# Row sums moved ahead of the remainder's product with v, and the order and PSUM banks of the score units written out by hand

## The chip, the cores and the metric

The kernel runs on one core of one Trainium2 chip. The metric is the device time of one execution in microseconds (us), the median of three runs. All engines of the core run at once: PE (TensorE, the matrix engine, with its weight loads shown as PEld), DVE (VectorE), ACT (ScalarE), POOL (GpSimd) and SP, which issues DMA transfers.

## The reference

Three stages follow one another; the change touches the first.

```
q_rot, k_rot = rotate(q), rotate(k)              # 4 batches x 8 heads, 576 positions, 64 wide
scores = q_rot @ k_rot^T / 8
attn   = exp(scores - max(scores)) / (sum(exp(scores - max(scores))) + 1e-9)
x      = attn @ v                                # heads side by side: 4 x 576 x 512
x      = moe(x)                                  # x @ w_in, gelu, spatial gate, @ w_out
out    = moe2(x)                                 # gated x @ w_val, @ w_out2
```

## The kernel before

**Attention.** The 32 heads are worked in 16 pairs, `i` = 0 to 15, one after the other. For a pair, PE first forms scores from which only the row maxima are taken, one pair ahead; then it forms the scores again, transposed, with the maximum subtracted inside the product, and ACT takes the exponential of each result straight out of PSUM.

One iteration of the loop in `attention()` has three parts on PE:

1. `phase(i)`: 16 units, in an order given by a string with one letter each. `t` (`st_unit`, lines 654 to 664) is 8 matmuls of pair `i` that make the scores of 128 keys times 288 queries for two heads; ACT's exponential (line 675) empties its bank. `T` (line 670) is the unit of the last 64 keys. `x` and `y` (`s_unit`, line 610) are score products of pair `i+1`, of four matmuls with 256 columns and of two matmuls with 320 columns; DVE's maximum (line 613) empties their bank. `S` (line 620) is the maximum unit of the last 64 queries, emptied by line 622. There are 8 `t`, 1 `T`, 2 `x`, 4 `y`, 1 `S`; the last pair has only the `t` and `T`.
2. `pv_unit` (line 699, eight matmuls in each of four calls): the product of the exponentials with v for the first 512 keys; then `pv_unit` with `(8,)` (line 709): the same for the 64 remaining keys. Both add into one bank, which ACT copies to `xu` (line 713, its copy shows as L263).
3. `sum_unit` (line 733): the row sums of the exponentials, by matmuls with ones, into another bank; ACT reads it into `ss` (line 737). Part of the addition is done ahead by POOL (`ac`, line 260).

**PSUM.** There are four buffers `PS[0]` to `PS[3]`, called banks here (each is in fact two banks wide, one for each head or half). Each unit of a phase takes one of them, and PE may write it only when the engine that empties it is done.

**What sets the order.** All work is put in a list of tasks. Tasks of PE run in exactly the order in which they are added; those of ACT, DVE, POOL and SP are ordered by a planner (class `Plan`) that lists them by modelled costs and due times. In `phase` a small model inside the loop (`free`, `pe`, `ac`, `dv`) chooses the bank for each unit. For the strings that stand there it gives plain rotation: banks 0, 1, 2, 3, 0, 1, ... for the phases 0 to 14 and 0, 1, 2, 0, 1, 2, ... for the last; the product with v is always in bank 3 and the row sums always in bank 2.

At the end of a phase and behind it, `prep_high(i+2)` lets DVE rotate the raw q and k of the pair after next; ACT casts them to `qp`, `qh` and `kh`, and the first `y` of the next phase needs `kh`.

**Behind attention** come the dense products of the two mixers (line 840), which take the time from about 236 us to the end.

Of the kernel before, what the change touches and what calls it, by code (L numbers as in the profile page):

```python
# [21 lines left out]
B, HP, S, DM, HALF = 4, 4, 576, 512, 288  # L22
NPAIR = B * HP
# [139 lines left out]
PASS = 0.132  # L163
MAXIMA = ((0.238, 1.14), (0.146, 0.75))
FP32 = 0.48
PART = 384
MORE = 4


@with_exitstack  # L170
def mixer_kernel(ctx: ExitStack, tc: tile.TileContext, qk, v, vrem, cs, w_in, g_ln, w_sgT, b_sg,
# [25 lines left out]
    PS = [psum.tile([128, 2, 512], F32, name=f"ps{j}") for j in range(4)]  # L197
# [64 lines left out]
    def acopy(out_, in_, n, r, w, after=()):  # L262
        return add("Act", act(n), lambda: nc.scalar.copy(out_(), in_()), r, w, after)  # L263
# [412 lines left out]
    def adds(i):  # L676
        return 4 if FOUR <= i < NPAIR - 1 else 2
# [8 lines left out]
            else:  # L686
                tt("P", lambda: AC[kc], lambda: AC[kc], lambda: E[n], ALU.add, S, [("e", n)], [("ac", kc)])

    def pv_unit(i, us):

        j2 = i % 2
        pv, kp = PS[3], ("ps", 3)
        if us[0] < 8:
            j = UNITS[us[0]][0]

            def mm():
                for h in range(2):
                    for hf in range(2):
                        nc.tensor.matmul(pv[64 * hf:64 * hf + 64, h, 0:HALF], VM[j2][:, j, h], E[EU[i, us[hf]]][:, h],  # L699
                                         start=j == 0, stop=False, skip_group_check=True)  # L700
            add("PE", 2 * FP32 + (0.2 if not j else 0.0), mm, [*[("e", EU[i, u]) for u in us], ("vm", j2)], [kp])
            return
        e = E[EU[i, 8]]

        def mm():
            for hf in range(2):
                for h in range(2):
                    rows = slice(64 * h, 64 * h + 64)
                    nc.tensor.matmul(pv[64 * hf:64 * hf + 64, h, 0:HALF], VR[j2][rows], e[rows, hf], start=False, stop=True,  # L709
                                     skip_group_check=True)  # L710
        add("PE", FP32 + 0.1, mm, [("e", EU[i, 8]), ("vr", j2)], [kp])
        xu = XU[j2]
        acopy(lambda: xu, lambda: pv[:, :, 0:HALF], S, [kp], [("xu", j2)])

        def st(q):
            for hf in range(2):
                q.dma_start(out=xu_d[i // HP][i % HP, :, HALF * hf:HALF * hf + HALF].rearrange("(h d) c -> d h c", h=2),
                            in_=xu[64 * hf:64 * hf + 64])
        dma(290, st, [("xu", j2)], [("xu_d", i)], n=2)

    def sum_unit(i, ps, kps):

        j2 = i % 2
        src = [(ones, ones, [(E[EU[i, u + hf]], h) for h in range(2) for hf in range(2)], ("e", EU[i, u]),
                ("e", EU[i, u + 1])) for u in (4, 6)[adds(i) // 2 - 1:]]
        src.append((ones, ones, [(AC[hf], h) for h in range(2) for hf in range(2)], ("ac", 0), ("ac", 1)))
        e = EU[i, 8]
        src.append((*ones_b, [(E[e], hf) for h in range(2) for hf in range(2)], ("e", e)))

        def mm():  # L730
            for n, x in enumerate(src):
                for t, (a, y) in enumerate(x[2]):
                    nc.tensor.matmul(ps[32 * t:32 * t + 32, 0, 0:HALF], x[t // 2], a[:, y], start=n == 0,  # L733
                                     stop=n == len(src) - 1, skip_group_check=True)
        add("PE", len(src) * FP32 + 0.15, mm, [*[k for x in src for k in x[3:]], ("consts",)], [kps])
        ss, rc = SS[0], RC[j2]
        add("Act", act(HALF), lambda: nc.scalar.activation(ss, ps[:, 0, 0:HALF], AF.Copy, bias=1e-9), [kps], [("ss", 0)])

        def rows(q):
            q.dma_start(out=rc, in_=ss[0:97:32].rearrange("t (p c) -> t p c", c=9))  # L740
        dma(5, rows, [("ss", 0)], [("rc", j2)])
# [22 lines left out]
    def attention():  # L764
        keep_busy(16)
        first_pairs()

        def phase(i, vl):

            order = "ytyttxtttyttyxTS" if i + 1 < NPAIR else "ttttttttT"  # L770
            if not i:
                order = "xtttyttytyttyxTS"
            free = [0.0, 0.0, 0.74 if i else 0.0, 0.0]
            pe, ac, dv = 0.2, 0.0, 0.0
            nt, xs, ys = 0, iter(range(2)), iter(range(2, 6))
            for x, what in enumerate(order):
                ks = range(4) if x < len(order) - 4 else range(3)
                at_once = [k for k in ks if free[k] <= pe]
                k = max(at_once, key=lambda k: free[k]) if at_once else min(ks, key=lambda k: free[k])
                pe = max(pe, free[k])  # L780
                if what in "tT":
                    pe += 4 * PASS if what == "t" else 8 * PASS + 0.24
                    act_at = max(ac, pe + 0.22)
                    ac, free[k] = act_at + 0.55, act_at + 0.75
                    st_unit(i, nt, PS[k], ("ps", k))
                    add_unit(i, nt)
                    nt += 1
                else:
                    pe += 2 * PASS if what == "S" else MAXIMA[what == "y"][0]
                    dve_at = max(dv, pe + 0.29)  # L790
                    dv = dve_at + (0.67 if what == "S" else MAXIMA[what == "y"][1])
                    free[k] = dv + 0.15
                    s_unit(i + 1, {"x": xs, "y": ys, "S": iter((8,))}[what].__next__(), PS[k], ("ps", k))
                if not x:
                    first = [P.last_pe, *vl]
                    if 2 <= i + 1 < NPAIR:
                        prep_low(i + 1, first)
                if x == (12 if i < FOUR else 0):
                    job_s(i, [P.last_pe])
            if i + 1 < NPAIR:  # L800
                s_end(i + 1)

        vl = []
        for i in range(NPAIR):
            if i + 2 < NPAIR:
                prep_load(i + 2)
            if i and i + 1 < NPAIR:
                load_v(i + 1)
            if i:
                job_loads(i)  # L810
            phase(i, vl)
            ep.append(P.last_pe)
            rot = [P.last_pe]
            if 0 < i < FOUR or i == NPAIR - 1:
                sum_end(i - 1, [*rot, *P.writer.get(("mn", (i + 1) % 2, 1), ())] if i + 1 < NPAIR else ())
            if i + 2 < NPAIR:
                rot = prep_high(i + 2, [P.last_pe, *P.writer[("mn", (i + 1) % 2, 1)]])
            vl = job_v(i, [P.last_pe], rot)
            if FOUR <= i < NPAIR - 1:
                sum_end(i - 1, P.writer["kl", (i + 1) % 3])  # L820
            for us in ((0, 2), (1, 3), (4, 5), (6, 7), (8,)):
                pv_unit(i, us)
            sum_unit(i, PS[2], ("ps", 2))
        sum_end(NPAIR - 1)

    def unit(cost, mm, r, new=True):
# [173 lines left out]
    def x2_part(b, dds=range(4)):  # L1000
        j = b % 2
        for dd in dds:
            dc = slice(128 * dd, 128 * dd + 128)
            x2t, kx = ((XS[0], ("xs", 0)), (XS[1], ("xs", 1)), (RB[0], ("rb", 0)), (RB[1], ("rb", 1)),
                       *((y, ("xm", y)) for y in range(MORE)))[nx[0] % (4 + MORE)]
            nx[0] += 1
# [29 lines left out]
    def val_part(b0):  # L1036

        for dd in range(4):
# [5 lines left out]
            def bank(y, z=z):  # L1044
                return PS[z[y // 2]][:, y % 2, 0:PART]

            for ks in ((0, 1), (2,), (3,)):
                def mm(dc=dc, bank=bank, ks=ks):
                    product(3, bank, lambda p, k, y: w2("v", p)[:, k, dc],
                            lambda q, k, y: (T["xh2"], T["xl2"])[q][:, k].rearrange("p a b -> p (a b)")[:, PART * y:PART * y + PART], ks=ks)  # L1050
                add("PE", len(ks) * 9 * 0.1735, mm, [("X2", j, k, m) for j in range(2) for k in ks for m in "hl"]
# [5 lines left out]
            for y in range(2):  # L1057
                n = (2 * PART, PART)[y]

                def part(y=y, n=n, gt=gt):  # L1060
                    return gt()[:, 2 * PART * y:2 * PART * y + n].rearrange("p (a b) -> p a b", b=PART)
                add("DVE", dve(n), lambda y=y, z=z, part=part: nc.vector.tensor_tensor(
                    part(), PS[z[y]][:, 0:2 - y, 0:PART], part(), ALU.mult), [("ps", z[y])], kg[y:])
            for j in range(2):
# [81 lines left out]
    def close_a():  # L1146
# [9 lines left out]
        T["ob"] = [p2.tile([128, 2, 512], F32, name=f"ob{j}") for j in range(2)]  # L1156
        T["xm"] = [p2.tile([128, 4 + S], F32, name=f"xm{j}") for j in range(MORE)]
        for t in T["xm"]:
# [6 lines left out]
        + [("YR", j, k, m) for j in range(B) for k in range(4) for m in "hl"] + [("ob", j) for j in range(2)]  # L1165
        + [("xm", j) for j in range(MORE)])})
    load_g(1)
# [73 lines left out]
```

## Time and profile before

| | us |
|---|---|
| median of 3 runs | 552.12 |
| lowest, highest | 551.88, 552.69 |
| time of the profiled execution | 552.56 |
| its span, first to last instruction | 550.8 |
| PE busy in it | 541.4 (98%) |
| DVE, ACT, POOL busy | 411.7, 278.4, 247.5 |

The span is counted within the profiled execution; the 1.76 us between span and time lie ahead of the first instruction and behind the last. Matmuls are pipelined, and each is shown longer than the distance to the next: a matmul of 288 columns is drawn as 0.29 us and the next pair starts 0.13 us later. PE that waits for a bank can therefore look busy all the while, and the distance from start to start has to be read.

### The profile page before, as it was taken

To read this page: it belongs to the slowest core of one execution; us is meant where nothing else is said; L and a number is where in the kernel's file an instruction comes from. 1 tells how busy PE (TensorE), PEld (TensorE's weight loads), DVE (VectorE), ACT (ScalarE), POOL (GpSimd) and SP (SyncE) were. 2 spreads that over 40 slices of the span, in tenths; PEclk is the share of its full clock that TensorE was granted. 3 is DMA by queue.
4 is the path that set the end of the run, shared out by engine and by line. 5 is a ranking of instruction groups with operands and counts; after the bars stand their busy time and mean duration, and the time that the engine had idled before them with its cause. 6 is when DMAs were issued, how large, how long until landed. Compare 5 with 4: busy or idle time off the path is not lost.

```text
span 550.8 us, 11758 instructions
## 1 busy us (share of the span) xinstructions
PE 541.4 (98%) x4592; PEld 463.3 (84%) x4592; DVE 411.7 (75%) x595; ACT 278.4 (51%) x451; POOL 247.5 (45%) x229
## 2 busy tenths in 40 slices
PE   6999999999999999999999999999999999999996
PEld 5877777777777777679989989989999998899985
DVE  7878888888888888969768556654979997649610
ACT  3567766776666667635526136134157543334221
POOL 5545555555555555456967677554610011222000
PEclk9999999999999999999999999999999999999999
DMA  5565656565666664774484762643264211110022
GB/s 187 141 195 142 184 152 175 160 185 153 188 171 160 168 198 103 214 223 111 131 295 119 231 189 75 196 142 124 104 208 128 73 44 72 44 58 1 0 77 96
DMA packets 58024, 77.39 MB, mean 141 GB/s; under 512 B 29392, under 2 KB 34000, under 8 KB 57968
## 3 DMA queue, kind: packets, MB, share of 16 engines
q1 hardware_dynamic: 57664, 76.37, 46.8%
q8 instruction: 36, 0.59, 0.4%
q10 hardware_dynamic: 304, 0.26, 0.1%
q14 instruction: 20, 0.16, 0.1%
HBM read 55.94 MB, written 18.95 MB: 136 GB/s over the span
## 4 chain that ended last, share of the span: by engine, by line
PE 96%; DVE 2%; DMA 1%; ACT 0%; issue 0%; SPq 0%; ACTq 0%; DVEq 0%
PE ps L840 55%; PE ps L662 12%; PE ps L699 12%; PE ps L733 6%; PE ps L670 4%; PE ps L610 4%; PE ps L709 2%; PE ps L951 2%; DVE raw L259 1%; DVE mx L613 1%; DMA raw<-qk 1%; PE ps L620 1%; DVE mn L622 0%; ACT ob L263 0%; ACT kh L263 0%
## 5 line engine op out<-in xcount | busy, mean ns | idle before, releaser
L613 DVE TENSOR_REDUCE mx<-ps 128x2 f32<-128x640 f32 (+1 forms) x96 | 89.1, 957 | 28.8 <-PE ps L610 21.9
L675 ACT ACTIVATE e<-ps 128x576 f32<-128x576 f32 x144 | 87.0, 652 | 20.3 <-PE ps L670 10.9
L699 PE MATMUL ps<-e,vm 128*64 128x288 f32 x512 | 65.6, 409 | 0.0
L699 PEld LDWEIGHTS ps<-e,vm 128*64 128x64 f32 x512 | 35.3, 137 | 24.7 <-issue 2.6
L260 POOL TENSOR_TENSOR ac<-e,e 128x576 f32<-128x576 f32 x32 | 45.2, 1431 | 9.4 <-ACT e L675 9.4
L840 PE MATMUL ps<-s_h,vn 128*128 128x288 f32 x256 | 46.9, 295 | 0.0
L259 DVE TENSOR_TENSOR raw<-raw,cst 128x1152 f32<-128x1152 f32 (+1 forms) x33 | 42.0, 1272 | 0.5 <-DMA raw<-qk 0.5
L263 ACT CAST qp<-raw 128x512 fp32r<-128x512 f32 x16 | 18.6, 1164 | 45.2 <-DVE raw L259 45.2
L840 PEld LDWEIGHTS ps<-s_h,vn 128*128 128x128 f32 x256 | 38.3, 188 | 0.0
L662 PE MATMUL ps<-qh,kh 64*128 64x288 f32 x256 | 38.3, 295 | 0.0
L662 PE MATMUL ps<-qh,kl 64*128 64x288 f32 x256 | 37.9, 292 | 0.0
L662 PE MATMUL ps<-ql,kh 64*128 64x288 f32 x256 | 37.8, 292 | 0.0
L662 PE MATMUL ps<-mr,one_r 64*128 64x288 f32 x256 | 37.7, 290 | 0.0
L260 POOL TENSOR_TENSOR vs<-vs,u 128x576 f32<-128x576 f32 x16 | 27.0, 1688 | 19.3 <-DVE vs L955 16.8
L610 PE MATMUL ps<-kh,qp 64*128 64x320 f32 (+1 forms) x256 | 32.7, 312 | 2.3 <-ACT kh L263 2.2
L1032 DVE SCALAR_TENSOR_TENSOR gt<-xm,cw,gt 128x576 f32<-128x576 f32 x32 | 28.9, 909 | 1.8 <-ACT gt L1029 1.4
L610 PEld LDWEIGHTS ps<-kh,qp 64*128 64x128 f32 x256 | 21.7, 184 | 10.0 <-ACT kh L263 7.7
L309 DVE TENSOR_SCALAR wt<-wt 128x256 f32<-128x256 f32 (+1 forms) x28 | 16.4, 586 | 16.5 <-ACT wt L319 16.5
L260 POOL TENSOR_TENSOR xl<-xs,xh 128x576 fp32r<-128x576 f32 x2 | 5.3, 2633 | 50.0 <-ACT xh L263 50.0
L840 PE MATMUL ps<-XL,w_h 128*128 128x288 f32 x128 | 27.4, 296 | 0.0
L840 PE MATMUL ps<-XH,w_l 128*128 128x288 f32 x128 | 27.4, 295 | 0.0
L840 PE MATMUL ps<-XH,w_h 128*128 128x288 f32 x128 | 27.4, 295 | 0.0
(181 smaller groups left out, 1493.4 us busy)
## 6 DMA issues: line engine op xcount, KB each, us to landing
raw<-qk SPq DMA_DIRECT2D x31, 576.0 KB
xu_d<-xu SPq DMA_DIRECT2D x32, 144.0 KB
rb<-r_d SPq DMA_DIRECT2D x32, 144.0 KB
xs<-xu_d SPq DMA_DIRECT2D x16, 288.0 KB
x_d<-xs SPq DMA_DIRECT2D x16, 288.0 KB
g_d<-vs SPq DMA_DIRECT2D x16, 288.0 KB
vm<-v SPq DMA_DIRECT2D x16, 256.0 KB
wr<-w_in SPq DMA_DIRECT2D x8, 512.0 KB
```

The lines of the kernel that those rows point to most:

```text
L259: return add("DVE", dve(n), lambda: nc.vector.tensor_tensor(out_(), a(), b(), op), r, w, after, lock=True)
L260: return add("Pool", pool(n), lambda: nc.gpsimd.tensor_tensor(out_(), a(), b(), op), r, w, after, lock=True)
L263: return add("Act", act(n), lambda: nc.scalar.copy(out_(), in_()), r, w, after)
L610: nc.tensor.matmul(ps[:, h, w * y:w * y + w], QP[j2][rows, c], kh[rows, keys], start=True, stop=True)
L613: add("DVE", MAXIMA[n // 2 > 0][1], lambda: nc.vector.tensor_reduce(out=MX[j2][:, n // 2 > 0, :, chunks[0]:chunks[-1] + 1], in_=ps[:, :, 0 ...
L662: nc.tensor.matmul(ps[:, h, 0:HALF], x[rows, keys] if o < 3 else x[rows], y[rows, cols], start=o == 0, stop=o == 3)
L670: nc.tensor.matmul(ps[:, hf, 0:HALF], x, y[:, cols], start=o == 0, stop=o == 3)
L675: add("Act", 0.62, lambda: nc.scalar.activation(E[n], ps[:, :, 0:HALF], AF.Exp), [kps], [("e", n)])
L699: nc.tensor.matmul(pv[64 * hf:64 * hf + 64, h, 0:HALF], VM[j2][:, j, h], E[EU[i, us[hf]]][:, h], start=j == 0, stop=False, skip_group_chec ...
L733: nc.tensor.matmul(ps[32 * t:32 * t + 32, 0, 0:HALF], x[t // 2], a[:, y], start=n == 0, stop=n == len(src) - 1, skip_group_check=True)
L840: nc.tensor.matmul(out_(y), lhs(p, k, y), rhs(q, k, y), start=not z, stop=ends and z == len(terms) - 1)
L1032: add("DVE", dve(S) + 0.05, lambda dd=dd, m=m, x2=x2, gt=gt: nc.vector.scalar_tensor_tensor(gt(), x2()[:, m:m + S], cw[:, 5 * dd + m:5 * d ...
```

## The change

The order of the units and the bank of each are written out in a table, one entry for the first phase, one for the phases 1 to 14, one for the last. The last two digits of an entry are the bank of the product with v and that of the row sums. The row sums are issued ahead of the product with v of the 64 remaining keys.

```diff
+ORDER = (("xtytytttyttytxTS", "123012302132102131"), ("ytyttyttxtttyxTS", "210320132013021030"), ("ttttttttT", "10231023102"))
...
-    def pv_unit(i, us):
+    def pv_unit(i, us, k):
...
-        pv, kp = PS[3], ("ps", 3)
+        pv, kp = PS[k], ("ps", k)
...
-            order = "ytyttxtttyttyxTS" if i + 1 < NPAIR else "ttttttttT"
-            if not i:
-                order = "xtttyttytyttyxTS"
-            free = [0.0, 0.0, 0.74 if i else 0.0, 0.0]
-            pe, ac, dv = 0.2, 0.0, 0.0
+            order, banks = ORDER[min(i, 1) if i + 1 < NPAIR else 2]
             nt, xs, ys = 0, iter(range(2)), iter(range(2, 6))
-            for x, what in enumerate(order):
-                ks = range(4) if x < len(order) - 4 else range(3)
-                at_once = [k for k in ks if free[k] <= pe]
-                k = max(at_once, key=lambda k: free[k]) if at_once else min(ks, key=lambda k: free[k])
-                pe = max(pe, free[k])
+            for x, (what, k) in enumerate(zip(order, banks)):
+                k = int(k)
...
-            for us in ((0, 2), (1, 3), (4, 5), (6, 7), (8,)):
-                pv_unit(i, us)
-            sum_unit(i, PS[2], ("ps", 2))
+            k, z = (int(y) for y in ORDER[min(i, 1) if i + 1 < NPAIR else 2][1][-2:])
+            for us in ((0, 2), (1, 3), (4, 5), (6, 7)):
+                pv_unit(i, us, k)
+            sum_unit(i, PS[z], ("ps", z))
+            pv_unit(i, (8,), k)
```

The lines of the small model that kept `pe`, `ac`, `dv` and `free` up to date go as well.

| unit | 0 | 1 | 2 | 3 | 4 | 5 | 6 | 7 | 8 | 9 | 10 | 11 | 12 | 13 | 14 | 15 | v | sums |
|---|---|---|---|---|---|---|---|---|---|---|---|---|---|---|---|---|---|---|
| phases 1 to 14, before | y0 | t1 | y2 | t3 | t0 | x1 | t2 | t3 | t0 | y1 | t2 | t3 | y0 | x1 | T2 | S0 | 3 | 2 |
| phases 1 to 14, after | y2 | t1 | y0 | t3 | t2 | y0 | t1 | t3 | x2 | t0 | t1 | t3 | y0 | x2 | T1 | S0 | 3 | 0 |
| phase 0, before | x0 | t1 | t2 | t3 | y0 | t1 | t2 | y3 | t0 | y1 | t2 | t3 | y0 | x1 | T2 | S0 | 3 | 2 |
| phase 0, after | x1 | t2 | y3 | t0 | y1 | t2 | t3 | t0 | y2 | t1 | t3 | y2 | t1 | x0 | T2 | S1 | 3 | 1 |

The digit is the bank. The last phase has its units in banks 1, 0, 2, 3, 1, 0, 2, 3, 1, the product with v in 0 and the sums in 2.

## Rows read from the trace of the kernel before

**Rows 1.** The page's head and its busy times.
```profile
span 550.8 us, 11758 instructions
...
PE 541.4 (98%) x4592; PEld 463.3 (84%) x4592; DVE 411.7 (75%) x595; ACT 278.4 (51%) x451; POOL 247.5 (45%) x229
```

**Rows 2.** Waits of PE: us in total, times, longest.
```profile
PE ps L610 <- ACT kh L263: 2.2, 2, 1.5
```

**Rows 3.** Timeline of PE, phase 7: start us, us, engine, line, operation, count.
```profile
115.83 0.41 PE L610 MATMUL ps<-kh,qp 64*128 64x320 f32 x2
...
116.62 0.31 PE L610 MATMUL ps<-kh,qp 64*128 64x320 f32 x2
116.76 0.30 PE L662 MATMUL ps<-qh,kh 64*128 64x288 f32 x2
...
117.82 0.39 PE L610 MATMUL ps<-kh,qp 64*128 64x256 f32 x4
...
119.64 0.37 PE L610 MATMUL ps<-kh,qp 64*128 64x320 f32 x2
119.86 0.30 PE L662 MATMUL ps<-qh,kh 64*128 64x288 f32 x2
```

**Rows 4.** Timeline of DVE in the same phase.
```profile
116.29 1.58 DVE L613 TENSOR_REDUCE mx<-ps 128x2 f32<-128x640 f32 x2 [0.32 <-PE ps L610]
118.32 1.23 DVE L613 TENSOR_REDUCE mx<-ps 128x4 f32<-128x1024 f32 x1 [0.45 <-PE ps L610]
```

**Rows 5.** Timeline of the weight loads, PEld, in the same phase.
```profile
119.60 0.19 PEld L610 LDWEIGHTS ps<-kh,qp 64*128 64x128 f32 x2
```

**Rows 6.** Timeline of PE, phase 0.
```profile
20.60 0.41 PE L610 MATMUL ps<-kh,qp 64*128 64x320 f32 x2
20.82 0.33 PE L662 MATMUL ps<-qh,kh 64*128 64x288 f32 x2
...
22.57 0.33 PE L610 MATMUL ps<-kh,qp 64*128 64x320 f32 x2
22.82 0.40 PE L662 MATMUL ps<-qh,kh 64*128 64x288 f32 x2
23.06 0.30 PE L662 MATMUL ps<-qh,kl 64*128 64x288 f32 x2
```

**Rows 7.** Timeline of ACT (first row) and DVE (second), phase 0.
```profile
19.34 0.44 ACT L263 CAST kh<-raw 128x288 fp32r<-128x288 f32 x1 [0.15 <-DVE raw L259]
...
19.23 1.22 DVE L613 TENSOR_REDUCE mx<-ps 128x4 f32<-128x1024 f32 x1
```

**Rows 8.** Timeline of PE (two rows) and ACT (one row), last phase.
```profile
225.63 0.34 PE L662 MATMUL ps<-qh,kh 64*128 64x288 f32 x2
225.81 0.29 PE L662 MATMUL ps<-qh,kl 64*128 64x288 f32 x2
...
224.86 1.20 ACT L675 ACTIVATE e<-ps 128x576 f32<-128x576 f32 x2 [0.33 <-PE ps L662]
```

**Rows 9.** Timeline of ACT between phases 6 and 7.
```profile
114.11 0.65 ACT L263 COPY xu<-ps 128x576 f32<-128x576 f32 x1
114.65 0.69 ACT L263 CAST kh<-raw 128x576 fp32r<-128x576 f32 x1
116.02 0.41 ACT L737 ACTIVATE ss<-ps 128x288 f32<-128x288 f32 x1 [0.69 <-ACT kh L263]
```

**Rows 10.** Timeline of PE, end of phase 6 and its products with v and sums.
```profile
108.73 0.42 PE L620 MATMUL ps<-kh,qr 128*128 128x288 f32 x2
109.08 4.10 PE L699 MATMUL ps<-e,vm 128*64 128x288 f32 x32
113.11 0.72 PE L709 MATMUL ps<-e,vr 64*64 64x288 f32 x8
113.76 1.18 PE L733 MATMUL ps<-e,ones 128*32 128x288 f32 x16
```

**Rows 11.** Timeline of POOL, phase 7.
```profile
119.02 2.79 POOL L260 TENSOR_TENSOR ac<-e,e 128x576 f32<-128x576 f32 x2
```

More of the change, by code (lines that the diff above doesn't have):

```diff
@@ L768, in phase @@
         def phase(i, vl):
-            order = "ytyttxtttyttyxTS" if i + 1 < NPAIR else "ttttttttT"
-            if not i:
-                order = "xtttyttytyttyxTS"
-            free = [0.0, 0.0, 0.74 if i else 0.0, 0.0]
-            pe, ac, dv = 0.2, 0.0, 0.0
-            nt, xs, ys = 0, iter(range(2)), iter(range(2, 6))
-            for x, what in enumerate(order):
-                ks = range(4) if x < len(order) - 4 else range(3)
-                at_once = [k for k in ks if free[k] <= pe]
-                k = max(at_once, key=lambda k: free[k]) if at_once else min(ks, key=lambda k: free[k])
-                pe = max(pe, free[k])
+            order, banks = ORDER[min(i, 1) if i + 1 < NPAIR else 2]
+            nt, xs, ys = 0, iter(range(2)), iter(range(2, 6))
+            for x, (what, k) in enumerate(zip(order, banks)):
+                k = int(k)
                 if what in "tT":
-                    pe += 4 * PASS if what == "t" else 8 * PASS + 0.24
-                    act_at = max(ac, pe + 0.22)
-                    ac, free[k] = act_at + 0.55, act_at + 0.75
                     st_unit(i, nt, PS[k], ("ps", k))
@@ L788, in phase @@
                 else:
[L789 to L792, printed above, removed]
                     s_unit(i + 1, {"x": xs, "y": ys, "S": iter((8,))}[what].__next__(), PS[k], ("ps", k))
```

## Prediction

> **What bounds the kernel now.** I read the page first: PE is busy for 98% of the span, every other engine for three quarters or less [rows 1]. So time is gained or lost where PE's stream is dense or not. The list of PE's waits is nearly empty and knows no wait for a bank [rows 2]; but matmuls are drawn longer than their distance, so this view can't show one that is shorter than a matmul. I therefore read PE's timeline from start to start, phase by phase, beside DVE, ACT and the weight loads.
>
> In phase 7 a `y` takes 0.14 us (116.62 to 116.76), two `t` take 1.06 us, 0.53 each (116.76 to 117.82) [rows 3]. But behind the `y` at 119.64 the next unit comes only after 0.22 us. The reason stands beside it: that `y` is in bank 1, as the `x` at 117.82 was; the maximum of this `x` ends at 118.32 + 1.23 = 119.55 [rows 4], and the weight load of the `y` starts at 119.60 [rows 5]. Two things are to be seen. A bank comes free for PE 0.05 us behind the end of its reader. And a weight load that starts late costs more than its lateness: the matmul of the `y` still starts in time, but the next unit starts 0.26 us behind the late load (119.60 to 119.86). So the rule that I use is: loss = load + 0.26 - when the next unit would have started. Here 119.60 + 0.26 - 119.79 = 0.07 us. I read this loss in 13 of the 14 phases 1 to 14.
>
> Phase 0 shows the same twice: 0.22 instead of 0.14 behind the `y` at 20.60, and a `t` that should start at 22.71, starts at 22.82 and whose second pair of matmuls comes 0.24 behind it instead of 0.13 [rows 6]: 0.11 late and 0.11 more for the load, 0.22 together. All the phase's losses are about 0.3 us. In the last phase, with three banks, the fourth `t` has 0.18 for 0.13 [rows 8]; its losses add up to about 0.09 us.
>
> **The change part by part.**
>
> *Banks, phases 1 to 14, gain.* The `y` that waited for the `x` is gone from that place; the new `x` (unit 8) is followed in its bank only by unit 13. 13 x 0.07 = 0.91 us.
>
> *Banks, phases 1 to 14, loss at unit 5.* Units 2 and 5 are now both `y` in bank 0, with two `t` between them. Units 0 to 4 have the same letters as before, so unit 2 keeps its place, 116.62 in phase 7, and DVE ends the two maxima of units 0 and 2 at 116.29 + 1.58 = 117.87 [rows 4]. DVE can't be earlier: unit 2's own matmuls end only at 116.93 [rows 3] and its maximum is a good 0.8 us long. Bank 0 is free at 117.92. Unit 5's matmul is due where the `x` stands now, at 117.82, and unit 6 at 117.82 + 0.15 = 117.97. By the rule unit 6 starts at 117.92 + 0.26 = 118.18: 0.21 us lost. The place of unit 2's maximum is the same in each of these phases, within 0.01 us. The loss can't fall below nothing, and not below 0.10 as long as the bank is free at 117.92; above I set 0.28, if unit 5 needs the further 0.05 that the first `y` row of phase 0 shows [rows 6]. I take 0.21, the same pattern.
>
> *Unit 3, behind the copy of the product with v.* This copy moves behind the remainder's product, now the last work of the iteration. ACT read the sums 0.19 us after the next phase's first matmul (116.02 against 115.83) [rows 3, 9]; the copy now takes that place with its 0.65 us [rows 9], so bank 3 is free at 0.19 + 0.65 + 0.05 = 0.89 in the phase. Unit 3 is due at 0.93 (116.76) and its second matmuls at 1.06: 0.89 + 0.26 - 1.06 = 0.09 lost. But this lies behind unit 2 and ahead of unit 5, whose bank comes free at a fixed time: unit 5 waits less by as much. It adds nothing until the copy is more than 0.1 late, and 0.09 a phase (1.3 us in all) if unit 5's wait isn't there.
>
> *Unit 12, after unit 9 in bank 0.* A `t`, two `t` between, then the bank again. That is the pattern of the last phase before, where it cost 0.18 - 0.13 = 0.05 [rows 8]. Bounds 0 and 0.07; I take 0.04.
>
> The other repeats in a bank are as far apart as before or further. Sum of these phases: 14 x (0.21 + 0.04) - 0.91 = +2.6 us.
>
> *Phase 0.* Unit 2 is now a `y` and due at 19.54, but needs the second half of `kh`, cast at 19.34 + 0.44 = 19.78 [rows 7]; load at 19.83, next unit at 20.09 instead of 19.69: 0.40. The first maximum ends at 20.45 [rows 7], so unit 2's ends about 21.23, and unit 6 in its bank, due at 21.29, loses about 0.11. Unit 11 after unit 8 is the pattern `y`, two `t`, `y` again: 0.21. Unit 12 follows unit 9 with one `t` and one `y` between: about 0.23, since the exponential that empties the bank ends 1.1 us behind the unit's last matmul, as in the last phase [rows 8], and only 0.9 lie between. Together 0.95, less the 0.3 lost today: +0.65 us (bounds 0 and 0.95).
>
> *Last phase.* Four banks in rotation instead of three: -0.09 us.
>
> *Row sums ahead of the remainder.* No matmul is added, so PE's work is the same: the remainder's 0.65 (113.11 to 113.76) and the sums change places [rows 10]. The sums' last inputs are there: POOL's additions of phase 7 end at 121.81 [rows 11], PE needs them some 6 us later. A change of the array's shape costs PE about 0.09 us: `S` to the product with v, where only the columns change, has 0.35 for two matmuls and the 0.13 of each [rows 10]. Before and after there are three such changes around the sums, so I count nothing. The read of the sums comes 0.65 us earlier and behind the cast of `kh`, whose input was there before [rows 9]; the bank of the sums is free long before unit 2. The store of `xu`, two issues on SP, goes about 1.9 us later and is read many phases on; the issue of the sums' transfer goes earlier. Both are hidden behind whole phases. If ACT took the sums ahead of `kh`, see below.
>
> At the late load a page speaks against the rule above. By the Trainium skill, "TensorE: Matmul & The Clock Gate", section "Step-by-step: what each phase is for", PE pulls weight loads ahead of running matmuls, so that the next weights come in behind them. If that hid the loads of units behind a waiting one, only the plain lateness would be lost. The trace doesn't bear it out: the wait of one `y` delays the unit behind it by the load as well.
>
> **Sum.** +2.6 + 0.65 - 0.09 = +3.15 us. The profiled execution took 552.56, which gives 555.7; it lies 0.44 above the median of the runs, so against that the forecast is 555.3.
>
> **Rivals.**
>
> *A. Only the lateness is lost, no weight load behind it.* Then unit 5 costs 0.10 and unit 12 nothing: 14 x 0.10 - 0.91 (measured, so it stands) + 0.2 in phase 0 - 0.09 = +0.6, that is 552.7. Against it stand both places in rows 3 and 6. Chance 0.10. It is what the page just named would make of it.
>
> *B. The shapes change more cheaply in the new sequence.* The last step to the next phase is from 64 rows to 64 rows (before from 128 to 64). If PE needed no change there, 0.09 for the change and 0.12 for the first load (115.83 to 116.62 is 0.79, 0.53 of it for the `t`, so 0.26 for the `y` instead of 0.14 [rows 3]) would be saved 15 times: about -3.0, that is 552.3, no change. It decides whether columns alone force a change; `S` to the product with v says they do [rows 10]. Chance 0.08.
>
> *C. No bank is late.* If the maxima gave up their banks 0.22 us sooner than I read, unit 5 would load in time; with the copy in time as well only the gains are left: -0.91 - 0.09 + 0.1 = -0.9, that is 551.2, at the edge of a gain. No row shows a bank handed over ahead of the end of its reader. Chance 0.09.
>
> *D. ACT's order turns.* If the planner put the read of the sums ahead of `kh`, the read would run from 116.02 - 0.65 = 115.37, `kh` behind it from about 115.73 to 116.42 [rows 9], and the first `y`, due at 115.83, would load at 116.47: 0.64 us late, 14 times, about +9, that is 564. For it speaks that the cast has no slack in the later phases; against it that it starts at 114.65, 0.7 us before the sums would be done. Chance 0.07.
>
> **How the numbers follow.** My forecast has a chance of 0.66, with a range of its own from 553.7 (unit 5 at 0.16, unit 12 at nothing, phase 0 at +0.3) to 556.5 (0.28, 0.05 and +0.75). The range reaches down to A and B and leaves C and D out: 552.3 to 556.5. About 0.2% (1.1 us) is what a measurement can tell from no change. Slower: the forecast and D, and a little of A, 0.75. The same: most of A, B and half of C, 0.18. Faster: the rest, 0.07.
>
> **What would show it.** In the phases 1 to 14 the distance from unit 5 to unit 6 should be about 0.26 to 0.36 instead of 0.15, the load of unit 5 should start 0.05 behind the end of unit 2's maximum, and the 0.22 behind the `y` after three `t` should be gone. The iteration of phase 7 should take 14.0 us from first matmul to first matmul, 13.83 before. Phase 0 should be 0.65 longer. I am wrong if unit 6 follows unit 5 at 0.15 (C), if the first `y` of a phase is followed at 0.14 (B), or if the first `y` itself waits for `kh` (D).

## The result, and the profile after

| | us |
|---|---|
| before, median (lowest, highest) | 552.02 (551.88, 552.69) |
| after, median (lowest, highest) | 555.87 (555.67, 557.53) |
| ratio, with its 95% interval | 1.0074 [1.0053, 1.0095] |
| profiled execution of after, its span | 555.67, 553.9 |

The change makes the kernel slower by 3.85 us in the medians and by 3.1 us from the one profiled execution to the other (553.9 - 550.8). That of before (552.56) lies above its median and that of after (555.67) is the lowest of its four, so the rows below account for 3.1 of the 3.85. The page of after has the same picture as [rows 1]: PE is busy nearly throughout, and 3.5 us longer, with as many matmuls.

```profile
span 553.9 us, 11796 instructions
...
PE 544.9 (98%) x4592; PEld 464.3 (84%) x4592; DVE 411.1 (74%) x595; ACT 280.7 (51%) x451; POOL 246.6 (45%) x229
```

Where the time lies is read from the first matmul of each stage. These are the rows of before, in PE's timeline: phase 0, phase 1, the last phase, the first dense product.

```profile
18.67 0.50 PE L610 MATMUL ps<-kh,qp 64*128 64x256 f32 x4 [0.70 <-ACT kh L263]
...
32.74 0.41 PE L610 MATMUL ps<-kh,qp 64*128 64x320 f32 x2
...
223.94 0.40 PE L662 MATMUL ps<-qh,kh 64*128 64x288 f32 x2
...
236.48 0.73 PE L840 MATMUL ps<-w_h,XH 128*128 128x512 f32 x2
```

And these are the same rows of after, with the end of the last phase's products (all lines of the changed kernel from 610 to 738 lie one further on than before).

```profile
18.37 0.50 PE L611 MATMUL ps<-kh,qp 64*128 64x256 f32 x4 [0.75 <-ACT kh L264]
...
33.02 0.41 PE L611 MATMUL ps<-kh,qp 64*128 64x320 f32 x2
...
226.33 0.40 PE L663 MATMUL ps<-qh,kh 64*128 64x288 f32 x2
...
237.54 0.67 PE L734 MATMUL ps<-e,ones_b 128*32 128x288 f32 x8
238.14 0.71 PE L710 MATMUL ps<-e,vr 64*64 64x288 f32 x8
239.62 0.73 PE L829 MATMUL ps<-w_h,XH 128*128 128x512 f32 x2 [0.77 <-ACT xu L264]
```

The differences of these starts, us, with the same reading of the kernels run as experiments (told below; the last column runs to the end of the span, which is given to 0.1 us):

| | start of phase 0 | phase 0 | phases 1 to 14 | last phase, to the dense products | dense products |
|---|---|---|---|---|---|
| before | 18.67 | 14.07 | 191.20 | 12.54 | 314.32 |
| after | 18.37 | 14.65 | 193.31 | 13.29 | 314.28 |
| e1 | 18.29 | 14.07 | 191.27 | 12.54 | 314.53 |
| e2 | 17.92 | 14.66 | 194.84 | 12.57 | 314.31 |
| e3 | 18.34 | 14.64 | 193.32 | 12.45 | 314.25 |
| e4 | 18.16 | 14.64 | 191.10 | 13.60 | 315.00 |
| e5 | 18.02 | 14.08 | 193.15 | 13.28 | 315.17 |
| e6 | 18.36 | 14.08 | 192.17 | 12.45 | 314.24 |
| e7 | 18.68 | 14.06 | 191.94 | 12.45 | 314.27 |
| e8 | 18.06 | 14.07 | 191.11 | 12.45 | 314.51 |
| e9 | 18.08 | 14.07 | 191.10 | 12.45 | 314.30 |
| e10 | 18.03 | 14.08 | 190.51 | 12.45 | 314.23 |
| e11 | 18.53 | 14.07 | 190.29 | 12.45 | 314.26 |

After against before: start -0.30, phase 0 +0.58, phases 1 to 14 +2.11, last phase +0.75, dense -0.04; together +3.1. The start moves between 17.92 and 18.68 over all these executions with no relation to the edits (e1, whose beginning is that of before, starts 0.38 earlier than before). I count it to the execution and not to the change. Of the +2.11, 0.24 is lost in phase 11 alone (13.73 us, where the phases 9, 10 and 12 of after have 13.49): its `T` starts late behind an exponential that is itself late. e3 and e4 have the same; why that exponential is late was not followed.

**Phase 7.** PE's timeline of after, to be held against [rows 3].

```profile
116.96 0.41 PE L611 MATMUL ps<-kh,qp 64*128 64x320 f32 x2
117.21 0.30 PE L663 MATMUL ps<-qh,kh 64*128 64x288 f32 x2
...
117.74 0.31 PE L611 MATMUL ps<-kh,qp 64*128 64x320 f32 x2
117.89 0.30 PE L663 MATMUL ps<-qh,kh 64*128 64x288 f32 x2
118.02 0.29 PE L663 MATMUL ps<-qh,kl 64*128 64x288 f32 x2
...
118.82 0.29 PE L663 MATMUL ps<-mr,one_r 64*128 64x288 f32 x2
119.05 0.41 PE L611 MATMUL ps<-kh,qp 64*128 64x320 f32 x2
119.30 0.30 PE L663 MATMUL ps<-qh,kh 64*128 64x288 f32 x2
...
122.06 0.30 PE L663 MATMUL ps<-mr,one_r 64*128 64x288 f32 x2
122.19 0.55 PE L611 MATMUL ps<-kh,qp 64*128 64x320 f32 x6
...
130.94 0.42 PE L611 MATMUL ps<-kh,qp 64*128 64x320 f32 x2
```

DVE's timeline of after in that phase, against [rows 4].

```profile
117.42 1.58 DVE L614 TENSOR_REDUCE mx<-ps 128x2 f32<-128x640 f32 x2 [0.32 <-PE ps L611]
```

The weight loads (PEld) of units 3, 5, 6 and 12, against [rows 5].

```profile
117.79 0.19 PEld L663 LDWEIGHTS ps<-qh,kh 64*128 64x128 f32 x2
...
119.05 0.19 PEld L611 LDWEIGHTS ps<-kh,qp 64*128 64x128 f32 x2 [0.17 <-DVE mx L614]
119.15 0.19 PEld L663 LDWEIGHTS ps<-qh,kh 64*128 64x128 f32 x2
...
122.09 0.44 PEld L611 LDWEIGHTS ps<-kh,qp 64*128 64x128 f32 x6
```

ACT's timeline of after around the start of the phase, against [rows 9].

```profile
115.68 0.67 ACT L264 CAST kh<-raw 128x576 fp32r<-128x576 f32 x1 [0.31 <-DVE raw L260]
116.50 0.41 ACT L738 ACTIVATE ss<-ps 128x288 f32<-128x288 f32 x1
117.09 0.64 ACT L264 COPY xu<-ps 128x576 f32<-128x576 f32 x1 [0.18 <-PE ps L710]
```

Four things are to be seen.

- Unit 5 is due at 118.82 + 0.13 = 118.95. Its bank's maximum ends at 117.42 + 1.58 = 119.00, the load starts at 119.05, the matmul too (0.10 late). Unit 6's own load comes only behind that, at 119.15, and unit 6 follows after 0.25 instead of 0.15. That is 0.20 lost.
- Unit 12 loads at 122.09 and still starts in time, 0.13 behind the matmuls before it: no loss.
- Unit 3's bank is free when the copy ends at 117.09 + 0.64 = 117.73; its load starts at 117.79, its second matmuls are in time, 0.13 behind the first. Lost: at most 0.02.
- The iteration takes 130.94 - 116.96 = 13.98 us, 13.83 before.

**The end.** PE's rows above show 238.14 to 239.62 = 1.48 us from the remainder's product to the first dense product, where [rows 10] have 0.65 behind a remainder: 0.83 us of waiting. ACT's timeline of after shows for what.

```profile
238.65 0.38 ACT L738 ACTIVATE ss<-ps 128x288 f32<-128x288 f32 x1
238.94 0.62 ACT L264 COPY xu<-ps 128x576 f32<-128x576 f32 x1
```

The product with v of the last pair is in bank 0. The first dense product takes bank 0 as well, and waits for this copy, which now comes behind the very last work of attention: 238.94 + 0.62 = 239.56, and the product starts at 239.62. Before, that product was in bank 3, and its copy kept nobody waiting.

### The profile page after: what moved, and what is told of

Read it like the earlier page. It is cut to its first block, busy times and chain, and to the rows that moved or that the text cites. A ratio compares the mean times of both kernels' runs of the same rounds, so it can differ in the third digit from the quotient of the medians.

```text
span 553.9 us, 11796 instructions
## 1 busy us (share of the span) xinstructions
PE 544.9 (98%) x4592; PEld 464.3 (84%) x4592; DVE 411.1 (74%) x595; ACT 280.7 (51%) x451; POOL 246.6 (45%) x229
## 4 chain that ended last, share of the span: by engine, by line
PE 96%; DVE 2%; ACT 1%; POOL 0%; issue 0%; ACTq 0%; POOLq 0%
PE ps L829 54%; PE ps L663 12%; PE ps L700 12%; PE ps L734 5%; PE ps L611 4%; PE ps L671 4%; PE ps L710 2%; PE ps L940 2%; PE ps L755 1%; DVE mx L614 1%; PE ps L621 1%; DVE raw L260 1%; ACT e L676 0%; DVE mn L623 0%; POOL mr L295 0%
## 5 line engine op out<-in xcount | busy, mean ns | idle before, releaser
L829 PE MATMUL ps<-s_l,vn 128*128 128x288 f32 x128 | 27.3, 294 | 0.0
```

The costliest lines, as they stand in the source:

```text
L829: nc.tensor.matmul(out_(y), lhs(p, k, y), rhs(q, k, y), start=not z, stop=ends and z == len(terms) - 1)
```

## Experiments

All kernels compute the whole reference. Ratios are to the kernel before, with 95% intervals.

**e1: the sums moved, nothing else.**

```diff
-            for us in ((0, 2), (1, 3), (4, 5), (6, 7), (8,)):
+            for us in ((0, 2), (1, 3), (4, 5), (6, 7)):
                 pv_unit(i, us)
             sum_unit(i, PS[2], ("ps", 2))
+            pv_unit(i, (8,))
```

> The kernel before with one part of the change alone: the row sums ahead of the remainder's product, old order and old banks. If the time is lost by the banks of the units (theory), the exchange costs next to nothing: the copy of the product with v ends 0.77 us into the next phase and unit 3 in its bank loses 0.02 to 0.09 us in 14 phases, so 552.2 to 553.3 against 552.0 before, and the wait of 0.07 behind the y after three t stays. If the moved sums are what costs (rival: shapes of the array, order on ACT), this kernel is at 554 or above; if the shapes change more cheaply, at 549.

552.58 us, 1.0011 [1.0002, 1.002], within the forecast. The phases are as before (14.07 and 191.27), also the end. So the new place of the sums costs nothing in the stages that it touches, and brings nothing: the 0.5 us of the medians lies in no stage of the profiled execution by more than 0.2 and isn't settled.

**e2: the table alone, the sums last.**

```diff
-            for us in ((0, 2), (1, 3), (4, 5), (6, 7)):
+            for us in ((0, 2), (1, 3), (4, 5), (6, 7), (8,)):
...
-            pv_unit(i, (8,), k)
```

> The changed kernel with the row sums put back behind the remainder's product; new order and new banks of the units stay. Theory: unit 5 still waits for the maximum of unit 2 in bank 0 and each of the phases 1 to 14 is 0.13 to 0.15 us longer than before (1.9 us), phase 0 0.5 us; the wait of 0.8 us at the first dense product is gone, because the copy of the last product with v then ends while the sums run. About 554.3. Rival (the sums' place is the cause): 552.0.

556.32 us, 1.0082 [1.0065, 1.0098]: a loss of that size is there without the moved sums, so their place isn't the cause. But the forecast, 554.3, was 2.0 us too low, and the account is another. The wait at the end is gone (12.57), and phases 1 to 14 are 1.5 us longer than in after. Two causes are in the rows. The banks of the table collide with sums that come last: PE's waits of e2 list a wait for the read of the sums, in phase 1, whose unit 1 has the bank of phase 0's sums.

```profile
PE ps L611 <- ACT kh L264: 1.1, 3, 0.7
PE ps L663 <- ACT ss L738: 0.2, 1, 0.2
```

And the first `y` behind each of the phases 9 to 12 comes late because `kh` does (13.70 to 13.95 us for these phases, in after mostly 13.49), which was new to me; e6 and e7 came upon it again, and e10 and e11 follow it up.

**e3: only the bank of the last product with v.**

```diff
-("ttttttttT", "10231023102")
+("ttttttttT", "10231023132")
```

> The changed kernel with one digit altered: the last pair's product with v in bank 3 instead of bank 0. Theory: the first dense product takes bank 0 and waits there for the copy that is now the last work of attention; in bank 3 it doesn't, so 0.8 us less than the changed kernel, 555.05. Rival: the dense product waits for something else that the later copy delays (its inputs, the order on ACT), then no change, 555.9.

554.64 us, 1.0048 [1.0033, 1.0063]: 1.23 below after in the medians, 0.9 by the spans, 0.84 in the last phase. PE's timeline of e3 at the end:

```profile
238.11 0.72 PE L710 MATMUL ps<-e,vr 64*64 64x288 f32 x8
238.75 0.73 PE L829 MATMUL ps<-w_h,XH 128*128 128x512 f32 x2
```

From the remainder to the dense product it is 0.64 again. ACT makes the copy even later here, from 239.62 to 240.25, and it costs nothing: the wait at the end was the bank's.

**e4: other banks for phases 1 to 14, same letters.**

```diff
-("ytyttyttxtttyxTS", "210320132013021030")
+("ytyttyttxtttyxTS", "210321032103120130")
```

> The changed kernel with the same order of units in the phases 1 to 14, but unit 5 in bank 1 and unit 6 in bank 0 (and the units behind them moved to fit). Theory: unit 5's bank was read by an exponential that ends 0.3 us earlier, so unit 5 waits for nothing, and unit 6, 0.15 us later, loses 0.06 to 0.08 instead of 0.20: 14 times 0.12 to 0.14, 1.7 to 2.0 us less than the changed kernel, 554.0. Rival (the order of letters or the moved sums cost, not the bank): no change, 555.9.

554.14 us, 1.0039 [1.0024, 1.0054], 1.73 below after. Phases 1 to 14 take 191.10, 2.2 less than in after. PE's timeline of e4 in phase 7 at unit 5:

```profile
117.74 0.30 PE L663 MATMUL ps<-mr,one_r 64*128 64x288 f32 x2
117.87 0.31 PE L611 MATMUL ps<-kh,qp 64*128 64x320 f32 x2
118.02 0.34 PE L663 MATMUL ps<-qh,kh 64*128 64x288 f32 x2
118.20 0.29 PE L663 MATMUL ps<-qh,kl 64*128 64x288 f32 x2
```

Unit 5 now comes in time, 0.13 behind the last matmuls, and unit 6 after 0.15; only its second matmuls are 0.05 late. With banks changed and no letter, the loss goes: it is a wait for the bank, and the order of the letters is harmless. The median gains less than these 2.2 us. In the profiled execution two other waits grew: the one at the end by 0.31, since ACT was still busy with a weight that had waited for a DMA transfer, and PE waited 0.46 us for POOL's `w_l` in the dense products. Neither lies in a stage that e4 edits.

**e5: the phase 0 of before in after.**

```diff
-("xtytytttyttytxTS", "123012302132102131")
+("xtttyttytyttyxTS", "012301230123012032")
```

> The changed kernel with the first phase's order and banks as they were. Theory: the new first phase loses its 0.5 us to a y that needs the second half of kh and to two repeats of a bank that come too soon; 0.5 us less than the changed kernel, about 555.3. Rival: the first phase is longer because the sums moved, then 555.9 stays.

555.32 us, 1.006 [1.0046, 1.0074]; phase 0 is 14.08, 0.57 less than in after. This part is as forecast, and the sums are still moved here, so the rival is out. The profiled execution as a whole gains only 0.14, since its dense products take 0.9 longer; 0.57 of that is a wait for `w_l` as in e4, the rest was not followed.

**e9: the three edits of e3, e4 and e5 together.**

> The changed kernel with all three places mended at once: old first phase, units 5 and 6 exchanged in their banks, last product in bank 3; the row sums stay first and the order of letters in phases 1 to 14 stays. Theory: the three losses are separate and add up, 0.55 + 1.8 + 0.8 to 1.2, so 552.4 to 552.8, the time of the kernel before or a little above. If something else of the change costs (rival), more than 553.2 is left.

551.75 us, 0.9996 [0.9987, 1.0005]. That is below the forecast of 552.4 to 552.8. By medians the single gains add up to 3.51 us (1.23 + 1.73 + 0.55) and the three together gave 4.12. By the stages of the table they add up within 0.01: phase 0, phases 1 to 14 and the last phase gain 0.58, 2.21 and 0.84, as they do one by one in e5, e4 and e3. The kernel is as fast as before: these three places are the whole loss that the stages show.

**e6 and e7: banks handed out by the time of their release.** A new order of the letters was to keep each bank's next use well behind its reader, with the sums ahead of the remainder (e6) or last (e7).

```diff
-ORDER = (("xtytytttyttytxTS", "123012302132102131"), ("ytyttyttxtttyxTS", "210320132013021030"), ("ttttttttT", "10231023102"))
+ORDER = (("xtttyttytyttyxTS", "012301230123012032"),
+         ("ytyttxtttyttxyTS", "012301230213021302"),
+         ("ytyttxtttyttxyTS", "312031203210321032"),
+         ("ttttttttT", "10231023132"))
```

> Row sums first as in the change, but order and banks chosen by the rule of the prediction so that almost no unit takes a bank that isn't free: phases 1 to 14 ytyttxtttyttxyTS in banks 0123012302130213, banks 0 and 3 exchanged in every second phase so that the bank of the copied product is unit 3's, the last phase in four banks with the product in bank 3, the first phase as before. Theory: no unit 9 loss (0.07), 0.02 to 0.05 left, the last phase 0.09 shorter, kh one wait shorter: 0.6 to 1.0 us less than the kernel before, 551.2. If the chain of the maxima to kh binds instead (rival: the maximum of S ends 0.1 us later against the phase's end), the gain of phases 9 to 14 is gone: 551.6. If banks aren't what counts, 552.6 as with the sums moved alone.

> The same with the row sums behind the remainder's product. Theory: the copy of the product with v stands ahead of the cast of kh on ACT again; in the phases from 9 on the first y waits up to 0.2 us for kh, 4 to 6 times, so 0.5 to 1.2 us slower than with the sums first: 552.0. Rival (the sums' place has no effect): the same time as with the sums first.

552.43 us, 1.0009 [1.0, 1.0018], and 552.62 us, 1.0011 [1.0002, 1.002]: both missed. The banks did what was expected, most of the phases 1 to 8 fell from 13.84 to 13.79 and 13.77. But phases 9 to 11 of e6 took 14.33, 13.85 and 13.60 where before has 13.35. PE's timeline of e6 at the start of phase 10 has the first `y` waiting for `kh`:

```profile
157.21 0.41 PE L614 MATMUL ps<-kh,qp 64*128 64x320 f32 x2 [0.49 <-ACT kh L267]
```

DVE's timeline of e6 six us earlier shows the rotation that feeds it (columns as in [rows 4]).

```profile
151.22 1.74 DVE L263 TENSOR_TENSOR raw<-raw,cst 128x1152 f32<-128x1152 f32 x1
...
153.66 1.35 DVE L263 TENSOR_TENSOR raw<-raw,cst 128x1152 f32<-128x1152 f32 x1
155.05 0.76 DVE L263 TENSOR_TENSOR raw<-raw 128x576 f32<-128x576 f32 x1
```

And POOL's timeline of e6 at the same moment:

```profile
150.93 0.81 POOL L264 TENSOR_TENSOR s_l<-xs,s_h 128x288 fp32r<-128x288 f32 x1
```

The same multiply takes 1.74 us in the first row and 1.35 in the second. Under the long one lies a subtraction of POOL, a preparation for the dense products that has nothing to do with the change; it runs from 150.93 to 151.74, 0.52 of it beside the multiply. In before, after, e1, e3, e4, e5, e8 and e9 none of these multiplies of attention is above 1.36. In e2, e6 and e7 it happened 4, 3 and 4 times. The chain from this multiply over the casts to the first `y` has little slack in the phases from 9 on: in e7 four multiplies that took 0.36 to 0.43 too long made the phases 9 to 12 longer by 0.23 to 0.42 than they are in e10.

In e6 more was lost in the phases 9 and 10, because ACT read the sums ahead of the cast of `kh`, which is rival D of the prediction. ACT's timeline of e6:

```profile
156.19 0.41 ACT L741 ACTIVATE ss<-ps 128x288 f32<-128x288 f32 x1 [0.67 <-ACT qh L267]
156.49 0.66 ACT L267 CAST kh<-raw 128x576 fp32r<-128x576 f32 x1
```

What `kh` is cast from was there at 155.05 + 0.76 = 155.81, but ACT stood idle for the sums, and the cast began 0.68 us later.

**e8: the new order up to phase 8, the old one behind.**

```diff
+ORDER = (("xtttyttytyttyxTS", "012301230123012032"),
+         ("ytyttxtttyttxyTS", "012301230213021302"),
+         ("ytyttxtttyttyxTS", "012301230123012032"),
+         ("ttttttttT", "10231023132"))
```

> A version meant to beat both: row sums last as before; phases 1 to 8 in the order ytyttxtttyttxyTS with banks 0123012302130213, where kh has half a microsecond of slack, phases 9 to 14 and the first phase as before, the last phase in four banks with the product in bank 3. Theory: 0.06 us less in each of eight phases and 0.09 in the last, 0.5 to 0.6 us less than the kernel before: 551.5. If the chain to kh binds already at the change from phase 8 to 9, 552.0. Rival (banks don't count): 552.0.

552.20 us, 1.0005 [0.9996, 1.0013]: missed. Behind phase 1, the new order's phases took 13.83 to 13.89, not 13.77. There the first maximum of a phase starts 0.07 later than in phase 1, and unit 4, in the bank of unit 0, loses that. A reciprocal of DVE (line 749) stands just ahead of this maximum in the even phases, but it isn't the cause: the odd phases are late without it, and e7 has it in the same place with maxima that start in time. What goes with the delay is the last reader of the first unit's bank. In all thirteen traces, the first maximum of a phase starts 0.53 us and not 0.46 behind the phase's first matmul exactly where ACT, and not DVE, emptied that bank last: in phases 2 to 9 of e8, whose first `y` has the bank of the product with v of the phase ahead, and in phase 1 of after, e2, e3, e4, e5 and e9. There the maximum waits for ACT beside PE, though ACT was done before. A bank changed for this alone wasn't tried.

**e10 and e11: e7 and e6 with the four subtractions of POOL held back** until `kl` is made, that is behind the rotations. The moved lines are the same in both.

```diff
     def job_s(i, ...):
...
-        if i in (9, 10):
-            cc = slice(HALF * (i - 9), HALF * (i - 8))
-            tt("P", lambda: s_l[:, 4, cc], ..., P.writer["ql", (i + 1) % 3])
-        if i in (11, 12):
...
     def job_v(i, after, rot):
...
             last = pool_waits(lambda: KL[j3].bitcast(F32)[0:1, S - 1:S], [("kl", j3)])
+        if i in (9, 10):
+            cc = slice(HALF * (i - 9), HALF * (i - 8))
+            tt("P", lambda: s_l[:, 4, cc], ..., last)
+        if i in (11, 12):
...
```

> The version with banks by release and row sums last, and with POOL's four subtractions of phases 9 to 12 (s_l, w_l) held back until kl is made, so that none runs beside DVE's rotation of the pair after next. Theory: with one beside it that multiplication took 1.71 to 1.78 us instead of 1.35 and kh, which has no slack there, came 0.3 to 0.4 us late four times; without, each stays at 1.35, the waits for kh (3.3 us with the start's) shrink by 1.0 to 1.5 and the time is 551.0 to 551.4. Rival (kh is late for another reason, the later maxima): multiplications at 1.35 and the waits stay, 552.6.

> The same for the version with the row sums first. Theory: no wait of 0.3 to 0.6 us for kh in phases 8 to 10, 1.2 to 1.8 us less than with the overlap, 550.8 to 551.2; between the two places of the row sums less than 0.5 us is left. Rival as above: 552.4.

551.26 us, 0.9985 [0.9976, 0.9994], and 551.18 us, 0.9982 [0.9974, 0.9991]. Both are as forecast, and below before and after. In e11 the multiply and the subtraction are apart; DVE's timeline:

```profile
151.37 1.35 DVE L263 TENSOR_TENSOR raw<-raw,cst 128x1152 f32<-128x1152 f32 x1
```

POOL's timeline of e11:

```profile
156.44 0.79 POOL L264 TENSOR_TENSOR s_l<-xs,s_h 128x288 fp32r<-128x288 f32 x1
```

PE's waits of e11 for `kh` have only the one at the start of phase 0 left:

```profile
PE ps L614 <- ACT kh L267: 0.7, 1, 0.7
```

Phases 1 to 14 went from 192.17 to 190.29 (e6 to e11) and from 191.94 to 190.51 (e7 to e10). ACT has the same order in e7 and e10, so the long multiplies were the reason for the miss of e7. Between e6 and e11 ACT's order turned back as well, with `kh` ahead of the sums, so the 1.88 us there are the work of both. What e11 gains over before in the phases 1 to 14 is 0.9 us: 0.05 in most of the phases 1 to 8 and from 9 on, and 0.36 in phase 13 (13.67 to 13.31), where in before the second matmul of `S` came 0.11 late and the next first `y` waited 0.20 for `kh`. e4 and e9 have 13.35 in that phase, so this part isn't owed to the new order alone.

## Why the prediction was right, and where it was not

The forecast of +3.15 came out at +3.1 between the profiled executions and at +3.85 in the medians; the median of after, 555.87, lies 0.57 above the 555.3 and within the range. The mechanism of the largest term was right. That the sum came so close is luck: errors of up to 0.83 us cancel in it.

- **The rule of the late load** (load + 0.26): right. Unit 5 lost 0.20 where 0.21 was forecast, with the load 0.05 behind the maximum and 0.25 to the next unit. Rival A, that only the lateness counts, is out: 0.10 late gave 0.20. Rival C is out too: the bank was not handed over sooner than its reader's end.
- **Unit 12**: mis-sized. 0.04 in each phase was taken from the last phase of before; its load was 0.03 late and cost nothing. That is 14 x 0.04 = 0.56 us too much. With the 0.01 a phase at unit 5 (0.14) and, the other way, the 0.24 of phase 11 that wasn't foreseen, it makes nearly all of the difference between the forecast +2.6 and the measured +2.11.
- **Unit 3 behind the copy**: forecast 0.09, hidden by unit 5's wait. It lost at most 0.02, since the copy began 0.13 and not 0.19 into the phase. e4, where unit 5 no longer waits, shows that little is behind it: 13.82 to 13.85 in its phases 2 to 8.
- **Phase 0**: +0.65 forecast, +0.58 measured. Its first y's wait for `kh` cost the forecast 0.40, as PE's timeline of after shows:

```profile
19.11 0.29 PE L663 MATMUL ps<-mr,one_r 64*128 64x288 f32 x2
19.54 0.41 PE L611 MATMUL ps<-kh,qp 64*128 64x320 f32 x2
19.79 0.29 PE L663 MATMUL ps<-qh,kh 64*128 64x288 f32 x2
```

  The `y` is due at 19.24 and starts at 19.54, 0.30 late, and the next unit 0.10 more behind it. Unit 6 lost 0.05 (0.11 forecast), units 11 and 12 together 0.34 (0.44). Not foreseen was unit 14, the `T`, in the bank of unit 11. PE's timeline of after has it 0.41 behind the `x`, where before has 0.33 (0.47 behind a `y` and an `x`, 0.14 of it the `y`'s):

```profile
24.33 0.40 PE L611 MATMUL ps<-kh,qp 64*128 64x256 f32 x4
24.74 0.40 PE L671 MATMUL ps<-qh,krh 128*128 128x288 f32 x1
```

  DVE's timeline of after has the maximum that keeps its bank until 24.68:

```profile
23.86 0.82 DVE L614 TENSOR_REDUCE mx<-ps 128x2 f32<-128x640 f32 x1 [0.51 <-PE ps L611]
```

  0.40 + 0.05 + 0.34 + 0.08, less the 0.3 lost before, gives 0.57; measured is 0.58.
- **Sums ahead of the remainder, counted as nothing**: right in the phases (e1: 14.07 and 191.27). Rival B, a cheaper change of shape, is out: the first `y` of phase 7 is followed after 0.25 us in after (116.96 to 117.21), as before. Rival D did not come about in after; the cast of `kh` ran ahead of the read of the sums. In e6 it did come about, in two phases.
- **The last phase**: here the step failed. I wrote that the later copy is hidden "behind whole phases". Behind the last pair there is no phase. The table's bank 0 for its product with v, the dense product's first bank and the moved copy make a wait of 0.83 us which the prediction doesn't have; e3 removes it with one digit. The units of that phase gained the 0.09 of the forecast (12.45 in e3, 12.54 before).

So +0.83 was missed. Without the start, the stages give +3.40 against +3.15, because the 0.56 too much at unit 12 stands against it; an execution that began 0.30 earlier did the rest. The 0.45 us by which the medians are further apart than these stages lie in no row. The three losses were each removed by a digit or an entry of the table, and the stages of e9 show none left.

## What to carry to other kernels

When banks are handed out by hand, write next to each unit when its bank's last reader ends, and look at the unit behind it as well: here 0.10 us of a late bank cost 0.20, because the next unit's weights were loaded late too. Follow each moved reader to its last iteration, where what hides it in the loop is gone, and see which buffer the next stage takes first. Where a bottleneck engine looks busy without a gap, read start to start; the list of waits had nothing of the largest loss in PE's rows, and the weight loads showed it.

## What the runs showed of the hardware that was not expected

A DVE multiply of 128x1152 with two inputs in SBUF takes 1.35 us, and 1.62 to 1.78 when a subtraction of POOL with two inputs in SBUF runs beside it. The overlap sets the price: 0.41 us of it (e2) cost 0.27, 0.52 (e6) cost 0.39, 0.58 (e7) cost 0.43, about 0.7 of the overlap each time. The subtraction began first in every case and took no longer than apart: for 128x288, 0.79 to 0.81 us beside a multiply and 0.79 to 0.80 in e10 and e11. DVE's and POOL's rows of e2 for the first of these numbers, DVE first:

```profile
194.78 1.62 DVE L260 TENSOR_TENSOR raw<-raw,cst 128x1152 f32<-128x1152 f32 x1
```

```profile
194.46 0.73 POOL L261 TENSOR_TENSOR w_l<-wf,w_h 128x256 fp32r<-128x256 f32 x1
```

By the Trainium skill, "SBUF — State Buffer", section "Who interferes with whom", a DVE instruction with two inputs in SBUF contends with a GpSimd instruction that reads SBUF, through a port pair that they share. The runs agree that they contend, and e10 and e11 show that it goes when the two are kept apart. What an overlap costs is taken from the rows above.
